# Half of the first product of blocks 3 to 6 as two units of seven block products, with q' and part of k' on ScalarE half a block sooner

## The chip, the cores and the metric

The kernel runs on one core of a Trainium2 chip. The metric is the device time of one execution in microseconds, of which less is better. The engines of the core have queues of their own that run in order: TensorE (PE; its weight loads are listed apart as PEld), VectorE (DVE), ScalarE (ACT), GpSimd (POOL) and SyncE (SP, which only issues DMAs here).

## The reference

Eight batch entries ("blocks" 0 to 7) of 576 tokens go through a linear attention with eight heads of 64, and then through a feed-forward layer of width 2048:

```python
def phi(x, c, s):
    r = np.maximum(x, 0.0)
    return np.concatenate([r * c, r * s], axis=-1)
q_p = phi(q, cos_w, sin_w)          # cos and sin of pi/2 * pos / 576
k_p = phi(k, cos_w, sin_w)
kv = np.einsum('bhsf,bhsd->bhfd', k_p, v)
z = np.sum(k_p, axis=2)
num = np.einsum('bhsf,bhfd->bhsd', q_p, kv)
den = np.einsum('bhsf,bhf->bhs', q_p, z)[..., None] + 1e-06
x = num / den                        # then tokens x 512
...
h = x @ w_in                         # 512 -> 2048: the first product
g = h * (1.0 / (1.0 + np.exp(-1.702 * h)))
out = g @ w_out                      # 2048 -> 512: the second product
```

Inputs and output are float32; matmuls take bfloat16 operands and add up in float32.

## The kernel before, in words

A block is worked in two stages, with the attention of the block after it (`nb`) laid between their matmuls.

**First product.** 512 of a block's tokens (64 of each block go into a common tail, `xt`) are multiplied by `w_in` in 16 chunks of 128 features: `mm1` (L373) is four matmuls of 512 columns into a PSUM bank (L365) and a GELU on ScalarE into `gT` (L371). Near its end `kv_next` (L711) makes k'v of the next block (72 small matmuls, L237) and VectorE copies it out as `kvs` (L245).

**Second product.** It is written as seven products of half-size blocks (`PRODUCTS`, L481) in place of eight: `wino_mm` (L508) does one half of one product, eight matmuls of 256 columns (L519), fourteen times a block. VectorE makes the sums of `g` that they need (`g_sums`, L466) and joins results (`join`, L538); ScalarE copies three of them out (`keep`, L527: "kept" p1, u2, p5) and the last, p4 (L586). Between the halves stand the numerators of the next block (`x_next`, L883: `num_mm` on TensorE, L310, `num_div` on VectorE, and a transposing DMA into `xT`, L354), five a block. The output leaves by DMAs on POOL's queue.

**Operands of the attention.** q' and k' are relu times a weight by position: an instruction with the cosine and one with the sine for each piece. `trig` (L161) does one of nine pieces of k' (128 x 256), `trig_q` (L176) one of five chunks of q' (128 x 512), each on VectorE or, with `act=True`, on ScalarE (L167, L183). A chunk of q' is then turned by a transposing DMA on SP's queue into `qT` (`qturn_dma`, L217). `vcopy` (L187) casts v. In blocks 2 to 6, all of this stood at the start of the first product, on VectorE.

**Units.** In the last block the first product is already done by seven block products in place of eight: class `Unit` (L642). A unit covers four chunks of features; its steps 1, 2, 6, 7, 5, 4, 3 are four matmuls of 256 columns each (L657) into three banks A, Bk and Bp. After steps 1, 6 and 7 ScalarE copies bank A out (`snap`, L669), and the next step into A waits for this copy; after steps 2, 5 and 3 VectorE adds a copy and a bank (`add`, L664); GELUs read the sums. Units need sums of `w_in` (`win_sum`, L614) and of x (`x_sum`, L631).

The order of all instructions is the order in which the kernel's code issues them (a manual schedule). PSUM banks go round: four of pool `pmm`, and two double ones of pool `pat`.

Of the kernel before, what the change touches and what calls it, by code (L numbers as in the profile page):

```python
# [20 lines left out]
def kernel(  # L21
# [230 lines left out]
                         start=first, stop=last)  # L252

    def ksum_rows():
        st["row"] = small.tile([2, 512], BF16, name="row", bufs=1)
        nc.vector.tensor_copy(st["row"], st["ks"][0:2])

    def ksum_turn():
# [27 lines left out]
    def div_half(a):  # L286
        pv = nums["ps"][a][:, 0:260].rearrange("p (h e) -> p h e", h=4)
        inv = small.tile([128, 4], F32, name="invh")
        nc.vector.reciprocal(inv, pv[:, :, 64])
        xn = small.tile([128, 4, 64], BF16, name="xh")  # L290
        nc.vector.tensor_tensor(xn, pv[:, :, 0:64],
                                inv.unsqueeze(2).to_broadcast([128, 4, 64]), op=MUL)
        nums[0, a] = [nums["ps"][a], xn]
# [71 lines left out]
            nc.tensor.matmul(hp[fc][:, t0:t1], wcol(kc, fc), x[b][:, kc, t0:t1],  # L365
                             start=(kc == 0), stop=(kc == KC - 1))

    def gelu(fc):
        if fc % 4 == 0:
            gT[fc // 4] = gpool.tile([128, 4, MT], BF16, name="g")  # L370
        nc.scalar.activation(gT[fc // 4][:, fc % 4], hp.pop(fc), AF.Gelu_apprx_sigmoid)  # L371

# [5 lines left out]

    xt = one.tile([128, KC, B * 64], BF16, name="xt")
    gt = one.tile([128, FC, B * 64], BF16, name="gt")  # L380

    gt5 = gt.rearrange("p f (a b t) -> p f a b t", a=2, t=32)

    def mm1_tail_first(half):
        hps = pmm.tile([128, 8, 64], F32, name="mm")
        for f in range(8):
            for kc in range(KC):
                nc.tensor.matmul(hps[:, f], wcol(kc, half * 8 + f), xt[:, kc, 0:64],  # L388
                                 start=(kc == 0), stop=(kc == KC - 1))
        nc.scalar.activation(gt5[:, ts(half, 8), :, 0], hps.rearrange("p f (a t) -> p f a t", a=2),  # L390
                             AF.Gelu_apprx_sigmoid)

    def mm1_tails(fc):
        hps = pmm.tile([128, MT], F32, name="mm")
# [89 lines left out]
    OPENS = ("p1", "p2", "p5")  # L484
    bank = {}
    kept = {}

    banks = {"main": {}, "tail": {}}

# [10 lines left out]
            banks[which][n, "all"] = t.rearrange("p (c d) -> p c d", c=2) if one_bank else None  # L500

    def wino_open():
        for n in ("w", "x", "y"):
            t = pmm.tile([128, 2, HD], F32, name="mm")
            bank[n] = [t[:, c] for c in range(2)]
            bank[n, "all"] = t
# [18 lines left out]
        eng.dma_start(out=dst[:, 2 * i + c0:2 * i + c1, ts(n, HD)], in_=t[:, c0:c1])  # L525

    def keep(n, src, act=True):  # L527
        kept[n] = ypool.tile([128, 2, HD], F32, name=f"kept_{n}", bufs=1)
        parts = [(kept[n], bank[src, "all"])]
        if bank[src, "all"] is None:  # L530
            parts = [(kept[n][:, c], bank[src][c]) for c in range(2)]
        for o, i in parts:
            if act:
                nc.scalar.activation(o, i, AF.Identity)  # L534
            else:
                nc.vector.tensor_copy(o, i)
# [74 lines left out]
        slot_no[0] += 1  # L611
        return slots[slot_no[0] % 8].rearrange("p (f t) -> p f t", f=2)

    def win_sum(n, i):  # L614
        tt = nc.vector.tensor_tensor
        o = {m: ws[m][:, :, ts(i, 512)] for m in ws}
        a = {(0, k): w_in_t[i][:, ts(k, 2), :] for k in range(2)}
        a.update({(1, k): w_in_t[2][:, ts(k, 2), ts(i, 512)] for k in range(2)})
        if n == "s1":
            tt(o[n], a[1, 0], a[1, 1], op=ADD)  # L620
        elif n == "s2":
            tt(o[n], o["s1"], a[0, 0], op=SUB)
        elif n == "s3":
            tt(o[n], a[0, 0], a[1, 0], op=SUB)
        else:
            tt(o[n], a[0, 1], o["s2"], op=SUB)

    def x_blk(b, k, t):
        return x[b][:, ts(k, 2), ts(t, 256)]

    def x_sum(b, n):  # L631
        tt = nc.vector.tensor_tensor
        if n == "t1":
            tt(xs[n], x_blk(b, 0, 1), x_blk(b, 0, 0), op=SUB)
        elif n == "t2":
            tt(xs[n], x_blk(b, 1, 1), xs["t1"], op=SUB)
        elif n == "t3":
            tt(xs[n], x_blk(b, 1, 1), x_blk(b, 0, 1), op=SUB)
        else:
            tt(xs[n], x_blk(b, 1, 0), xs["t2"], op=SUB)  # L640

    class Unit:  # L642
        def __init__(self, b, u, A, Bk, Bp):
            self.b, self.u = b, u
            self.A, self.Bk, self.Bp = [t.rearrange("p (f t) -> p f t", f=2) for t in (A, Bk, Bp)]

        def mm(self, to, a, t, opens):
            for j in range(2):
                fc = 2 * self.u + j
                for k in range(2):  # L650
                    if isinstance(a, str):
                        lhs = ws[a][:, k, ts(fc // 4, 512)].rearrange("p (f c) -> p f c", c=4)[:, :, fc % 4]
                    else:
                        lhs = wcol(2 * a[1] + k, 8 * a[0] + fc)
                    rhs = xs[t][:, k] if isinstance(t, str) else x_blk(self.b, *t)[:, k]

                    nc.tensor.matmul(to[:, j], lhs, rhs, start=(opens and j == 0 and k == 0), stop=(k == 1),  # L657
                                     skip_group_check=True)
# [3 lines left out]
            nc.scalar.activation(o, i, AF.Gelu_apprx_sigmoid)  # L662

        def add(self, i, j):  # L664
            o = slot()
            nc.vector.tensor_tensor(o, i, j, op=ADD)
            return o

        def snap(self, i):  # L669
            o = slot()  # L670
            nc.scalar.activation(o, i, AF.Identity)
            return o

        def step(self, p):
            if p == 1:
                self.mm(self.A, (0, 0), (0, 0), True)
                self.s1 = self.snap(self.A)
            elif p == 2:
                self.mm(self.Bk, (0, 1), (1, 0), True)
                self.c11 = self.add(self.s1, self.Bk)  # L680
            elif p == 6:
                self.mm(self.A, "s2", "t2", False)
                self.s2 = self.snap(self.A)
            elif p == 7:
                self.mm(self.A, "s3", "t3", False)
                self.s3 = self.snap(self.A)
            elif p == 5:
                self.mm(self.Bp, "s1", "t1", True)
                self.c22 = self.add(self.s3, self.Bp)
            elif p == 4:  # L690
                self.mm(self.A, (1, 1), "nt4", False)
            else:
                self.mm(self.Bp, "s4", (1, 1), False)
                self.c12 = self.add(self.s2, self.Bp)

    def idle(n, cols=512):
        w = pmm.tile([128, 512], F32, name="mm")
# [191 lines left out]
    for b in range(1, B):  # L889
# [1 line left out]
        if nb is None:  # L891
            break
        f0 = 5 if b == 1 else 0
        for fc in range(f0, FC):
            if nb is not None and fc == f0:
                for c in range(5):
                    trig_q(c)
                    qturn_dma(c)
            if nb is not None and fc == f0 + 1:
                kv_operands(nb)  # L900

                if nb + 1 < B:
                    if b == 1:
                        load(kf, k, nb + 1, nc.sync)
                    load_q(nb + 1, nc.sync)
            if fc == 8 and b == 1:
                vcopy()
            if fc == 12:
                if b > 1:
                    g_sums(("s3",), 0)  # L910
                    g_sums(("s3",), 1)
                g_sums(("s1", "s2", "s4") if b > 1 else ("s1", "s2"), 0)
            if fc == 14 and nb is not None and b > 1:
                kv_next()
            mm1(b, fc)
        if nb is not None:
            x_open(nb)
            if b > 1:
                x_next(nb, 0)
            else:  # L920
                kv_mm_next()
            g_sums(("s1", "s2"), 1)
            if b == 1:
                kv_evac(0, 4)
                g_sums(("s3",), 0)
# [3 lines left out]
            for p in range(7):  # L929
                for c in range(2):  # L930
                    wino_mm(p, c)
                    s = 2 * p + c
                    if c == 1:
                        wino_after(b, p)
                    for c2 in at.get(s, ()):
                        x_next(nb, c2)
                        if c2 == 3 and nb + 1 < B:
                            if b > 1:
                                load(kf, k, nb + 1, nc.sync)
                            load(vf, v, nb + 1, nc.sync)  # L940
                    if s == 1 and b > 1:
                        g_sums(("s4",), 1)
                    if s == 2 and b == 1:
                        g_sums(("s3",), 1)
                    if s == 4 and b == 1:
                        g_sums(("s4",), 0)
                    if s == 6 and b == 1:
                        g_sums(("s4",), 1)

    b = B - 1
    for o, i in later:
        nc.gpsimd.dma_start(out=o, in_=i)
    for fc in range(FC):
# [99 lines left out]
```

## Time and profile before

| | us |
|---|---|
| median of 3 runs | 277.93 (277.73 to 277.98) |
| profiled execution, whole time | 277.36 |
| its span in the profile | 275.6 |
| one block, 2 to 6, from chain of waits | 28.6 |
| first product of a block, 64 matmuls of 512 columns | 13.9 |
| second product, 112 matmuls of 256 columns | 12.2 |
| granted TensorE clock | 0.999 |

The span is the time from the first to the last recorded instruction; the whole time has what lies around it too. The page lists busy time by engine and by group of instructions ("line engine op out<-in xcount | busy, mean ns of one | idle before"). The mean of one is longer than the distance between the starts of two, because an engine overlaps instructions that follow one another; distances are read from the timeline.

### The profile page before, as it was taken

Reading aid. Unit: us, or ns where it says so; the run is one execution under the profiler, and the core shown is the slowest. Engines: PE = TensorE matmul, PEld = TensorE weight load, DVE = VectorE, ACT = ScalarE, POOL = GpSimd, SP = SyncE. Lnnn points to the kernel's source line nnn. Section 1 sums busy time; section 2 is a strip of 40 time slices with the busy share of each in tenths; the row PEclk is TensorE's granted clock in tenths of the full one; section 3 lists DMA queues with packets and bytes.
Section 4 is the critical chain, followed back from the end, with each engine's and each line's share of the span. In section 5 each row is a group of like instructions: output and inputs, shape, how many; then the busy total and the mean of one; then the engine's idle time right before and its main releaser. Section 6 shows DMA issues by size and latency. Waiting matters only on the chain.

```text
span 275.6 us, 6720 instructions
## 1 busy us (share of the span) xinstructions
PE 269.3 (98%) x2748; PEld 195.0 (71%) x2748; DVE 199.4 (72%) x478; ACT 133.9 (49%) x237; POOL 41.3 (15%) x70
## 2 busy tenths in 40 slices
PE   7899999999999999999999999999999999999994
PEld 2685645856975698559855895589648976999983
DVE  4843776698899686978698759875987783744741
ACT  6967642574226512652165216621563147677621
POOL 6690000000130012001210012002200162000310
PEclk9999999999999999999999999999999999999999
DMA  7999999999999988998899969978991353000333
GB/s 240 250 211 298 276 293 153 281 300 200 286 213 223 218 170 257 274 171 191 241 285 176 211 194 351 176 190 125 365 245 26 88 167 118 0 2 0 84 109 114
DMA packets 73661, 53.57 MB, mean 194 GB/s; under 512 B 52736, under 2 KB 63488, under 8 KB 73632
## 3 DMA queue, kind: packets, MB, share of 16 engines
q1 hardware_dynamic: 67504, 36.97, 59.6%
q0 software_dynamic: 6128, 16.19, 22.2%
q8 instruction: 21, 0.34, 0.5%
q14 instruction: 8, 0.07, 0.1%
HBM read 36.70 MB, written 9.44 MB: 167 GB/s over the span
## 4 chain that ended last, share of the span: by engine, by line
PE 93%; DMA 4%; DVE 1%; ACT 0%; issue 0%; POOL 0%
PE mm L365 35%; PE mm L519 31%; PE mm L421 5%; PE mm L657 4%; PE at L519 4%; PE mm L396 4%; PE at L237 4%; PE at L310 3%; DMA sums<-in_v_dram 2%; DMA kf<-in_k_dram 1%; PE at L342 1%; PE mm L388 1%; DVE xn L325 1%; PE mm L205 0%; ACT xT L349 0%
## 5 line engine op out<-in xcount | busy, mean ns | idle before, releaser
L365 PE MATMUL mm<-xT,w_in 128*128 128x512 bf16 (+1 forms) x528 | 99.8, 345 | 0.0
L371 ACT ACTIVATE g<-mm 128x512 bf16<-128x512 f32 x112 | 66.0, 598 | 34.8 <-PE mm L365 34.8
L365 PEld LDWEIGHTS <-w_in 128*128 128x128 bf16 x528 | 53.0, 113 | 40.4
L519 PEld LDWEIGHTS <-sums 128*128 128x128 bf16 x448 | 42.5, 98 | 4.7
L525 POOL DMA_DIRECT2D out_dram<-ysb x24 | 17.4, 725 | 183.0 <-DVE den L321 85.4
L519 PE MATMUL mm<-wsum,sums 128*128 128x256 bf16 x336 | 39.9, 272 | 0.0
L519 PEld LDWEIGHTS <-g 128*128 128x128 bf16 x336 | 32.0, 98 | 3.6
L325 DVE TENSOR_TENSOR xn<-at,inv 128x512 bf16<-128x512 f32 x39 | 27.0, 692 | 1.3
L169 DVE TENSOR_SCALAR kr<-kf,cosw 128x256 bf16<-128x256 f32 x69 | 24.1, 349 | 5.2 <-DMA kf<-in_k_dram 5.2
L519 PE MATMUL mm<-w_out_sb,g 128*128 128x256 bf16 x224 | 26.6, 273 | 0.0
L169 DVE TENSOR_SCALAR kr<-kf,sinw 128x256 bf16<-128x256 f32 x68 | 23.0, 339 | 0.0
L534 ACT ACTIVATE kept_p<-mm 128x512 f32<-128x512 f32 (+1 forms) x15 | 8.5, 569 | 20.0 <-PE mm L519 20.0
L185 DVE TENSOR_SCALAR qn<-qf,cosw 128x512 bf16<-128x512 f32 (+1 forms) x33 | 16.4, 497 | 2.3 <-DMA qf<-in_q_dram 2.3
L321 DVE TENSOR_SCALAR den<-at 128x8 f32<-128x8 f32 x36 | 5.9, 163 | 16.5 <-PE at L310 16.5
L586 ACT ACTIVATE ysb<-mm 128x512 f32<-128x512 f32 x6 | 3.6, 598 | 29.0 <-PE mm L519 29.0
L310 PEld LDWEIGHTS <-qT 128*128 128x128 bf16 x312 | 14.3, 97 | 2.4
L310 PE MATMUL at<-kvs,qT 128*128 128x65 bf16 x312 | 15.7, 193 | 0.0
L185 DVE TENSOR_SCALAR qn<-qf,sinw 128x512 bf16<-128x512 f32 (+1 forms) x33 | 15.6, 474 | 0.0
L534 ACT ACTIVATE kept_u<-mm 128x512 f32<-128x512 f32 (+1 forms) x8 | 4.4, 544 | 23.2 <-DVE xn L325 16.8
L421 PE MATMUL mm<-w_out_sb,g 128*128 128x512 bf16 x64 | 14.8, 379 | 0.0
L519 PE MATMUL mm<-wsum,g 128*128 128x256 bf16 x112 | 13.4, 273 | 0.0
L519 PE MATMUL mm<-w_out_sb,sums 128*128 128x256 bf16 x112 | 13.4, 273 | 0.0
(147 smaller groups left out, 319.9 us busy)
## 6 DMA issues: line engine op xcount, KB each, us to landing
kf<-in_k_dram SPq DMA_DIRECT2D x6, 1152.0 KB, 6.3
vf<-in_v_dram SPq DMA_DIRECT2D x6, 1152.0 KB, 11.2
qf<-in_q_dram SPq DMA_DIRECT2D x6, 1024.0 KB, 6.8
out_dram<-ysb POOLq DMA_DIRECT2D x24, 256.0 KB, 7.1
w_out_sb<-in_moe_w_out_dram POOLq DMA_DIRECT2D x4, 512.0 KB, 17.6
kf<-in_k_dram POOLq DMA_DIRECT2D x1, 1152.0 KB, 13.4
vf<-in_v_dram POOLq DMA_DIRECT2D x1, 1152.0 KB, 20.7
w_in<-in_moe_w_in_dram POOLq DMA_DIRECT2D x2, 512.0 KB, 10.0
```

The costliest lines, as they stand in the source:

```text
L169: eng.tensor_scalar(o, i, 0.0, w[:, j:j + 1], op0=MAX, op1=MUL)
L185: nc.vector.tensor_scalar(o, i, 0.0, sc, op0=MAX, op1=MUL)
L237: nc.tensor.matmul(st["kv", i][:, hh, ds(col, n)], kr[r, j, i, :], rhs(r, i, j), start=(j == 0), stop=(j == NS - 1))
L310: nc.tensor.matmul(ps[:, h // 4, ds((h % 4) * 65, 65)], qT[:, h, ts(c, 128)], kvs_of(h), start=not eps_too, stop=(not eps_too or h % 4 == ...
L325: nc.vector.tensor_tensor(xn, pv[:, :, :, 0:64], inv.unsqueeze(3).to_broadcast([128, 2, 4, 64]), op=MUL)
L365: nc.tensor.matmul(hp[fc][:, t0:t1], wcol(kc, fc), x[b][:, kc, t0:t1], start=(kc == 0), stop=(kc == KC - 1))
L371: nc.scalar.activation(gT[fc // 4][:, fc % 4], hp.pop(fc), AF.Gelu_apprx_sigmoid)
L396: nc.tensor.matmul(hps[:, 64:B * 64], wcol(kc, fc), xt[:, kc, 64:B * 64], start=(kc == 0), stop=(kc == KC - 1))
L421: nc.tensor.matmul(yp[b, t, c0][:, c0:c1], w, w_out_sb[:, fc, c0:c1], start=(fc == 0), stop=(fc == FC - 1))
L519: nc.tensor.matmul(bank[to][c], lhs, rhs, start=opens, stop=(fc == HF - 1), skip_group_check=True)
L525: eng.dma_start(out=dst[:, 2 * i + c0:2 * i + c1, ts(n, HD)], in_=t[:, c0:c1])
L534: nc.scalar.activation(o, i, AF.Identity)
```

## The change

In blocks 3 to 6 (`PAIR`) `mm1_pair` takes the place of the sixteen `mm1`. Chunks 4 to 7 and 12 to 15 stay whole; chunks 0 to 3 and 8 to 11 are done by two units, U and V, with steps laid between the whole chunks. Six chunks use a bank of `pat`, two of `pmm`. The sums of `w_in` for the units are made once, in block 2, in the space of `gt`; so the first block's tail goes to `gt0` and is copied into `gt` by POOL at the end. The sums of x are made on VectorE behind the second product of the block before. The units' copies lie in `gt` and in the three kept buffers, which are now fixed.

q' moves from the start of the first product, on VectorE, to ScalarE behind half products 8 to 12 of the second product before it (from block 1 on), with its transposing DMAs; two of nine pieces of k' move with it (for blocks 4 to 7); the other seven are laid between the units' steps. The load of kf comes with that of qf in the first product. Some `g_sums` move.

```diff
@@ gelu, mm1_tail_first
-    def gelu(fc):
-        if fc % 4 == 0:
+    def gelu(fc, units=False):
+        if fc % 4 == 0 and not units:
             gT[fc // 4] = gpool.tile([128, 4, MT], BF16, name="g")
...
+    gt0 = one.tile([128, FC, 64], BF16, name="gt0")
...
-        nc.scalar.activation(gt5[:, ts(half, 8), :, 0], hps.rearrange("p f (a t) -> p f a t", a=2),
-                             AF.Gelu_apprx_sigmoid)
+        nc.scalar.activation(gt0[:, ts(half, 8)], hps, AF.Gelu_apprx_sigmoid)
@@ wino_open
-        for n in ("w", "x", "y"):
+        for n in ("w", "y", "x"):
@@ new
+    PAIR = range(3, B - 1)
...
+    def x_pair(b):
+        t = xpool.tile([128, KC, MT], BF16, name="xT")
+        xp[b] = {n: t[:, i].rearrange("p (k t) -> p k t", k=2) for i, n in enumerate(("t1", "t2", "t3", "nt4"))}
+        for n in xp[b]:
+            x_sum(b, n, xp[b])
+
+    def mm1_at(b, fc):
+        hp[fc] = pat.tile([128, 2, 512], F32, name="at")[:, 0]
+        for kc in range(KC):
+            nc.tensor.matmul(hp[fc], wcol(kc, fc), x[b][:, kc], start=(kc == 0), stop=(kc == KC - 1))
+        gelu(fc, True)
+
+    def mm1_pair(b, nb):
+        for qd in (0, 2, 1, 3):
+            gT[qd] = gpool.tile([128, 4, MT], BF16, name="g")
+        banks4 = [pmm.tile([128, 512], F32, name="mm") for _ in range(4)]
+        U, V = [Unit(b, u, banks4[u], banks4[2], banks4[3], ws_pair, xp[b], pair_slot) for u in range(2)]
+        ks = iter(range(2, NS))
+
+        def k_next(n):
+            for _ in range(n):
+                trig(kr, kf, next(ks))
+
+        U.step(1)
+        V.step(1)
+        k_next(2)
+        mm1_at(b, 4)
+        mm1_at(b, 5)
+        U.step(2)
+        k_next(3)
+        U.step(6)
+        V.step(6)
+        U.gelu(0, 0, U.c11)
+        mm1_at(b, 6)
+        mm1_at(b, 7)
+        V.step(2)
+        k_next(1)
+        U.step(7)
+        U.step(5)
+        V.gelu(0, 0, V.c11)
+        k_next(1)
+        V.step(7)
+        mm1_at(b, 12)
+        U.gelu(1, 1, U.c22)
+        U.step(4)
+        U.gelu(1, 0, U.A)
+        vcopy()
+        if nb + 1 < B:
+            load(kf, k, nb + 1, nc.sync)
+            load_q(nb + 1, nc.sync)
+        U.step(3)
+        V.step(4)
+        V.gelu(1, 0, V.A)
+        U.gelu(0, 1, U.c12)
+        mm1_at(b, 13)
+        g_sums(("s3",), 1)
+        V.step(5)
+        mm1_part(b, 14, 0, MT)
+        V.gelu(1, 1, V.c22)
+        V.step(3)
+        gelu(14)
+        kv_next()
+        mm1_part(b, 15, 0, MT)
+        V.gelu(0, 1, V.c12)
+        gelu(15)
+        g_sums(("s1", "s2"), 0)
@@ the loop over blocks
+        if b in PAIR:
+            mm1_pair(b, nb)
-        for fc in range(f0, FC):
-            if nb is not None and fc == f0:
+        for fc in range(f0, FC) if b not in PAIR else ():
+            if b == 1 and fc == f0:
                 for c in range(5):
                     trig_q(c)
                     qturn_dma(c)
...
-                    if b == 1:
-                        load(kf, k, nb + 1, nc.sync)
+                    load(kf, k, nb + 1, nc.sync)
                     load_q(nb + 1, nc.sync)
+                if b == 2:
+                    for n in ws_pair:
+                        win_sum(n, 0, ws_pair)
...
             g_sums(("s1", "s2"), 1)
+            if b > 2:
+                x_next(nb, 0)
...
                         if c2 == 3 and nb + 1 < B:
-                            if b > 1:
-                                load(kf, k, nb + 1, nc.sync)
                             load(vf, v, nb + 1, nc.sync)
-                    if s == 1 and b > 1:
+
+                    if s > 7 and s < 13 and nb + 1 < B:
+                        trig_q(s - 8, act=True)
+                        qturn_dma(s - 8)
+                        if s > 10 and nb in PAIR:
+                            trig(kr, kf, s - 11, act=True)
+                    if s == 1 and b == 2:
                         g_sums(("s4",), 1)
+                    if s == 1 and b > 2:
+                        g_sums(("s3",), 0)
+                    if s in (2, 4) and b > 2:
+                        g_sums(("s4",), s // 2 - 1)
...
+            if nb in PAIR:
+                x_pair(nb)
...
+    nc.gpsimd.tensor_copy(gt5[:, :, :, 0], gt0.rearrange("p f (a t) -> p f a t", a=2))
     for o, i in later:
```

More of the change, by code (lines that the diff above doesn't have):

```diff
@@ L254, in ksum_rows @@
     def ksum_rows():
-        st["row"] = small.tile([2, 512], BF16, name="row", bufs=1)
+        st["row"] = wsum[0:2, 1, 0:512]
         nc.vector.tensor_copy(st["row"], st["ks"][0:2])
@@ L289, in div_half @@
         nc.vector.reciprocal(inv, pv[:, :, 64])
-        xn = small.tile([128, 4, 64], BF16, name="xh")
+        xn = small.tile([128, 4, 64], BF16, name="xh", bufs=2)
         nc.vector.tensor_tensor(xn, pv[:, :, 0:64],
@@ L486 @@
     kept = {}
+    kept_t = {n: one.tile([128, 2, HD], F32, name=f"kept_{n}") for n in ("p1", "u2", "p5")}
     banks = {"main": {}, "tail": {}}
@@ L527, in keep @@
     def keep(n, src, act=True):
-        kept[n] = ypool.tile([128, 2, HD], F32, name=f"kept_{n}", bufs=1)
+        kept[n] = kept_t[n]
         parts = [(kept[n], bank[src, "all"])]
@@ L612, in slot, with win_sum @@
         return slots[slot_no[0] % 8].rearrange("p (f t) -> p f t", f=2)
-    def win_sum(n, i):
+    def win_sum(n, i, ws=ws):
         tt = nc.vector.tensor_tensor
@@ L629, in x_blk, with x_sum @@
         return x[b][:, ts(k, 2), ts(t, 256)]
-    def x_sum(b, n):
+    def x_sum(b, n, xs=xs):
         tt = nc.vector.tensor_tensor
@@ L642, with __init__ @@
     class Unit:
-        def __init__(self, b, u, A, Bk, Bp):
-            self.b, self.u = b, u
+        def __init__(self, b, u, A, Bk, Bp, ws=ws, xs=xs, slot=slot):
+            self.b, self.u, self.ws, self.xs, self.slot = b, u, ws, xs, slot
             self.A, self.Bk, self.Bp = [t.rearrange("p (f t) -> p f t", f=2) for t in (A, Bk, Bp)]
@@ L651, in mm @@
                     if isinstance(a, str):
-                        lhs = ws[a][:, k, ts(fc // 4, 512)].rearrange("p (f c) -> p f c", c=4)[:, :, fc % 4]
+                        lhs = self.ws[a][:, k, ts(fc // 4, 512)].rearrange("p (f c) -> p f c", c=4)[:, :, fc % 4]
                     else:
                         lhs = wcol(2 * a[1] + k, 8 * a[0] + fc)
-                    rhs = xs[t][:, k] if isinstance(t, str) else x_blk(self.b, *t)[:, k]
+                    rhs = self.xs[t][:, k] if isinstance(t, str) else x_blk(self.b, *t)[:, k]
                     nc.tensor.matmul(to[:, j], lhs, rhs, start=(opens and j == 0 and k == 0), stop=(k == 1),
@@ L664, in add @@
         def add(self, i, j):
-            o = slot()
+            o = self.slot()
             nc.vector.tensor_tensor(o, i, j, op=ADD)
@@ L669, in snap @@
         def snap(self, i):
-            o = slot()
+            o = self.slot()
             nc.scalar.activation(o, i, AF.Identity)
@@ L694, in step, with pair_slot @@
                 self.c12 = self.add(self.s2, self.Bp)
+    PAIR = range(3, B - 1)
+    gt_flat = gt.rearrange("p f e -> p (f e)")
+    ws_pair = {n: gt_flat[:, ts(i, 1024)].rearrange("p (k f) -> p k f", k=2)
+               for i, n in enumerate(("s1", "s2", "s3", "s4"))}
+    pair_slots = [gt_flat[:, 4096:8192].bitcast(F32)[:, ts(i, 512)] for i in range(4)]
+    pair_slots += [kept_t[n].rearrange("p c d -> p (c d)") for n in ("p1", "u2", "p5")]
+    pair_no = [0]
+    xp = {}
+    def pair_slot():
+        pair_no[0] += 1
+        return pair_slots[pair_no[0] % 7].rearrange("p (f t) -> p f t", f=2)
@@ L917 @@
             x_open(nb)
-            if b > 1:
+            if b == 2:
                 x_next(nb, 0)
-            else:
+            if b == 1:
                 kv_mm_next()
             g_sums(("s1", "s2"), 1)
+            if b > 2:
+                x_next(nb, 0)
             if b == 1:
@@ L937 @@
                         if c2 == 3 and nb + 1 < B:
-                            if b > 1:
-                                load(kf, k, nb + 1, nc.sync)
                             load(vf, v, nb + 1, nc.sync)
-                    if s == 1 and b > 1:
+                    if s > 7 and s < 13 and nb + 1 < B:
[4 more added lines that the diff above has]
+                    if s == 1 and b == 2:
                         g_sums(("s4",), 1)
+                    if s == 1 and b > 2:
+                        g_sums(("s3",), 0)
+                    if s in (2, 4) and b > 2:
+                        g_sums(("s4",), s // 2 - 1)
                     if s == 2 and b == 1:
```

## The prediction

> **What bounds the kernel now.** I read the page first, then the chain that ended last, then the timeline of each engine over one block, and last the waits.
>
> ```profile
> span 275.6 us, 6720 instructions
> PE 269.3 (98%) x2748; PEld 195.0 (71%) x2748; DVE 199.4 (72%) x478; ACT 133.9 (49%) x237; POOL 41.3 (15%) x70
> ```
>
> TensorE is busy all the time, so only fewer or shorter matmuls can gain. The chain, in order of time (start, length, what), shows it for block 3; the last line is from block 7, where the unit products exist already:
>
> ```profile
> 108.95 12.09 PE mm L365 x56
> 121.04 1.19 PE at L237 x72
> 122.23 1.85 PE mm L365 x8
> 124.08 0.24 PE at L310 x8
> 124.32 1.75 PE mm L519 x16
> ...
> 132.28 5.24 PE mm L519 x48
> 137.52 12.09 PE mm L365 x56
> ...
> 237.94 0.87 PE mm L657 x8
> ```
>
> A block lasts 28.57 us (108.95 to 137.52) and TensorE has no hole in it: 13.94 us of first product, 1.19 of kv, five numerators of 0.24, 12.24 of second product. No stall waits to be removed; a new one is paid in full. The other engines, block 3, by windows (length, then PE, PEld, DVE, ACT, POOL busy, clock, DMA share):
>
> ```profile
> 108.95:137.52 28.57, 28.57 (x289) 20.49 (x288) 23.05 (x57) 11.94 (x20) 2.90 (x5) 1.00 1.01 225
> ```
>
> VectorE has 5.5 us free, ScalarE 16.6; the DMA engines are full most of the time.
>
> **The matmuls.** A 512-column matmul costs 12.09/56 = 0.216 us, a 256-column one 0.87/8 = 0.109 (L657; L519 has 12.24/112, the same). In blocks 3 to 6 the change replaces 32 of the first kind (6.91) by 2 units x 7 products x 4 = 56 of the second (6.12): 0.79 us less a block, 3.16 in all. The changed program's order on TensorE has these matmuls and nothing else new, so this part does what it says.
>
> Weight loads rise from 32 to 56. In block 7 they take 0.114 us (L657 on w_in, x48), a little more than the 0.109 at which their matmuls follow one another, and the chain shows no hole there: they overlap. The Trainium skill, "TensorE: Matmul & The Clock Gate", section Back-to-back issue gap, says that in a real stream load and matmul together set the spacing and gives 131 ns for 512 columns; the rows here say 216, so its figure does not hold in this kernel. By that figure (an estimate) the 32 matmuls would take 4.2 us, less than the 56 can, and the change could only lose. What its rule would do through the loads is a rival below.
>
> **The ScalarE queue, where I expect the answer.** The queue runs in order. Until now it held three copies and an output copy in the second product. Now, behind the copy "kept p5" (after half product 8 of 14), come 10 instructions of q' and 4 of k', then the output copy of p4, then the copy s1 of unit U, the copy of V, and the GELUs of chunks 4 and 5. TensorE may not start U's second product into bank A (step 6) before s1 is copied out. The rows for each piece, ScalarE's timeline:
>
> ```profile
> 8.32 0.49 ACT L167 ACTIVATE qn<-qf,cosw 128x256 bf16<-128x256 f32 x1
> 8.72 0.49 ACT L167 ACTIVATE qn<-qf,sinw 128x256 bf16<-128x256 f32 x1
> ...
> 35.15 0.72 ACT L183 ACTIVATE qn<-qf,cosw 128x512 bf16<-128x512 f32 x1 [1.01 <-DMA qf<-in_q_dram]
> 35.77 0.71 ACT L183 ACTIVATE qn<-qf,sinw 128x512 bf16<-128x512 f32 x1
> 36.38 0.71 ACT L183 ACTIVATE qn<-qf,cosw 64x512 bf16<-64x512 f32 x1
> ...
> 132.13 0.60 ACT L534 ACTIVATE kept_p<-mm 128x512 f32<-128x512 f32 x1 [1.40 <-PE mm L519]
> ...
> 238.04 0.60 ACT L534 ACTIVATE kept_p<-at 128x512 f32<-128x512 f32 x1 [1.65 <-PE at L519]
> 238.53 1.08 ACT L671 ACTIVATE qn<-mm 128x512 f32<-128x512 f32 x2
> ```
>
> Starts follow one another at 0.615 us (q', (36.38-35.15)/2), 0.40 (the k' form), 0.50 (a copy out of PSUM, 238.53-238.04). With t = 0 at the second product's start (124.32 in block 3):
> - ScalarE: kept p5 starts at 132.13-124.32 = 7.81; q' from 8.31; 10 x 0.615 = 6.15 and 4 x 0.40 = 1.60 bring the output copy to 16.06, s1 of U to 16.56, and its end (0.60) to 17.16.
> - TensorE: the second product ends at 137.52-124.32 = 13.20; step 1 of U and V (8 x 0.109), chunks 4 and 5 (8 x 0.216) and step 2 of U (0.44) bring it to 16.23.
>
> TensorE is 0.93 early. It then starts from a standstill:
>
> ```profile
> 46.74 0.70 DVE xn L325
> 47.45 0.05 issue
> 47.49 0.40 PE at L342 x4
> ```
>
> 0.05 for the signal, and the first 256-column matmul ends 0.27 after its start (L519's mean) where in the stream it is 0.11: 0.21 more. **This wait costs 1.14 us a block**, more than the 0.79 won.
>
> **Smaller waits behind it, per block.** V's step 6 and chunk 6 (it needs chunk 4's bank, freed by a GELU that ends at 17.56+0.60): 0.10. V's step 3 writes the bank that V's add must have read; the trip is 0.16 drain + 0.05 + 0.69 add (L666) + 0.05 = 0.95, with one chunk (0.86) to cover it: 0.09. U's add before V's step 5 stands behind the vcopy of 1.34: 0.09. One chunk, not two, now stands between kv and the numerators, and kvs needs 0.17 + 0.04 + 0.70 (L245) + 0.05 = 0.96: 0.10. Each is an estimate from the rows named, bounded by 0 and about twice its size; no gain is possible in them, since TensorE has no hole now. Sum 0.38.
>
> **What stays hidden.** VectorE loses q' (10 x 0.40) and four instructions of k' (4 x 0.26), and gets 6 adds at 0.60 and 4 sums at 0.42: about even, at most 24 of 28 us. The four sums come after the last join, about t = 12.1 to 13.8, 3 us before step 6 asks for them. win_sum (4 x 0.60, block 2) takes the place of q'. The clearing copy on POOL lies ahead of the late outputs, 9 us before the tail's sums read it. In SP's queue kf now goes out ahead of qf, half a block sooner, vf stays behind the fourth x transpose, and the qT transposes come behind vf instead of after it by a half block; qT is read a full first product later, so it has room. A second load issued behind the first landed 11.2 us after its issue (vf's row on the page). kf goes out when the last k' on VectorE is done, near t = 22.8, 6 us before the next second product; qf is then there about 5 to 6 us into it, and q' asks at 8.3. Cover 2 to 3 us; past it, each us is one us of wait in each of three or four blocks.
>
> **Block 2** keeps its chunks, but ScalarE also does q' in block 1's second product. qf's second part landed at 76.27 in the trace; 6.15 of q' and the output copy end at 83.0, and the fourth chunk asks for that bank at 80.30 + 3 x 0.864 = 82.9. Between 0 and 0.7; I take 0.2.
>
> **The sum.** 4 x (-0.79 + 1.14 + 0.38) + 0.2 = +3.1 us. The profiled execution took 277.36 (span 275.6 and 1.76 around it); it becomes 280.5. The median of the three runs is 277.93, 0.57 above that execution, so I predict 281.0.
>
> **Why q' is dear there.** VectorE does a q' instruction every 0.40 us (L185 in its timeline), ScalarE every 0.615. The Trainium skill, "ScalarE: Activation LUTs", section Rules for kernel authors, puts relu and multiply on VectorE for this reason; by this rule, which the rows bear out, the move loses. Its section on ACT_TABLE_LOAD adds that each [128,1] pointer operand costs about 93 ns; q' has its weight in one. An estimate from that page: with a plain number as scale the 14 instructions would be 1.3 us shorter and the wait gone. No row here shows such a form on q'.
>
> **Rivals.**
> - *ScalarE is in time* (faster). Mechanism: q' at t = 8.3 to 14.5 lies under the second product and s1 is out before 16.2. It decides at q' spacing: (16.23 - 0.60 - 8.31 - 1.60 - 0.50)/10 = 0.52 us. Below it the gain is 0.79 less 0.28 of the trips through VectorE, 4 x 0.51 = 2.0: 275.9. For: ScalarE's 16.6 free us. Against: three spacings at 0.61 to 0.63. Chance 0.11.
> - *Only the bare lateness counts*: 0.93 and nothing more, 4 x 0.14 = 0.6, 278.5. For: small waits often vanish in each other. Against: the restart shown above has both the 0.05 and the drain. 0.13.
> - *qf comes late* by 1 us past its cover: +4 on the forecast, 285. For: DMA share 1.01. Against: the cover of 2 to 3 us. 0.10.
> - *Weight loads bind*: unit matmuls at 0.114, not 0.109; 56 x 0.005 = 0.3 a block, 282.1. The rule of the TensorE page named above goes this way. Against: the 0.87 for 8 in block 7. 0.03.
> - The forecast has 0.63; its own range is 279.3 (the one wait alone) to 282.8 (small waits doubled).
>
> **How the numbers follow.** About 0.2% (0.56 us) is what a measurement can tell from no change. Faster 0.12: the first rival and a little for what I haven't seen. Same 0.08: over half of the second rival, which lies on the edge. Slower 0.80: the rest. The range 277.2 to 284.5 leaves out the first rival and half of the third, with what lies beyond: 0.18.
>
> **What the changed profile would show.** Right: the chain in blocks 3 to 6 no longer all TensorE, with ScalarE pieces (the trig lines, ysb, the copy s1) some 3 us after each second product; a TensorE hole near 1 us in front of step 6, and a block of 29.2 to 29.4 us. Unit products at 0.87 for 8. Wrong on the main step: kept p5 to s1 under 8.4 us, or no hole there; wrong in another way if q' waits for qf, or if the hole stands in front of step 1.

## The result, and the profile after

| | before | after |
|---|---|---|
| median, run alternately | 277.89 (277.59 to 277.98, 5 runs) | 280.86 (280.48 to 280.94, 5 runs) |
| profiled execution, whole time | 277.36 | 280.48 |
| one block, 3 to 6 | 28.57 | 29.23 to 29.30 |
| granted TensorE clock | 0.999 | 1.00 in every block |

The changed kernel takes 1.0101 times as long (95% interval 1.0088 to 1.0113): 2.97 us slower by the medians, 3.12 by the profiled executions, of which 2.9 lie in the span. The page of the changed kernel, span and engines:

```profile
span 278.5 us, 6996 instructions
PE 268.9 (97%) x2844; PEld 204.7 (74%) x2844; DVE 198.2 (71%) x456; ACT 177.5 (64%) x327; POOL 43.0 (15%) x71
```

PE is busy 0.4 us less, although the span is 2.9 longer: TensorE now has holes. ScalarE has 43.6 us more work. The chain that ended last, which used to run through all blocks on TensorE, now breaks off, followed back, at a ScalarE piece in front of block 6's step 6:

```profile
200.22 0.49 ACT gt L672
200.71 0.04 issue
200.75 1.08 PE mm L658 x8
201.83 1.77 PE at L721 x8
203.60 1.75 PE mm L658 x16
```

`gt` (L672) is the copy s1 of unit U, and the eight matmuls behind it are step 6 of U and of V. The last line settles the weight loads: 16 unit matmuls in 1.75 us are 0.109 each, as forecast. Who releases TensorE, by its waits (total, times, longest):

```profile
PE mm L658 <- ACT gt L672: 1.8, 2, 0.9
PE mm L658 <- ACT kept_p L672: 1.7, 2, 0.9
```

Four waits in four blocks, all on copies by `snap`. Block by block, in windows from step 6 to the next step 6 (length, then PE, PEld, DVE, ACT, POOL busy, clock, DMA share, GB/s):

```profile
112.93:142.16 29.23, 28.37 (x312) 22.91 (x312) 22.91 (x53) 21.44 (x41) 2.90 (x5) 1.00 0.97 211
142.16:171.46 29.30, 28.38 (x313) 22.90 (x312) 22.83 (x53) 21.44 (x41) 2.91 (x5) 1.00 0.85 220
171.46:200.75 29.29, 28.38 (x312) 22.92 (x312) 22.82 (x53) 21.43 (x41) 2.90 (x5) 1.00 0.92 211
```

ScalarE is busy 21.4 of 29.3 us in the block, so it is by no means full; what counts is when its work stands in its queue. ScalarE's timeline, from the copy kept p5 to s1, in front of block 3:

```profile
103.60 0.60 ACT L535 ACTIVATE kept_p<-mm 128x512 f32<-128x512 f32 x1 [1.40 <-PE mm L520]
104.10 0.71 ACT L183 ACTIVATE qn<-qf,cosw 128x512 bf16<-128x512 f32 x1
104.71 0.71 ACT L183 ACTIVATE qn<-qf,sinw 128x512 bf16<-128x512 f32 x1
...
111.42 0.49 ACT L167 ACTIVATE kr<-kf,sinw 128x256 bf16<-128x256 f32 x1
111.82 0.57 ACT L587 ACTIVATE ysb<-mm 128x512 f32<-128x512 f32 x1
112.30 1.06 ACT L672 ACTIVATE gt<-mm 128x512 f32<-128x512 f32 x2
```

From kept p5 to s1 it takes 112.30 - 103.60 = 8.70 us (forecast 16.56 - 7.81 = 8.75), without a gap. TensorE's timeline in the same block:

```profile
111.43 0.60 PE L658 MATMUL mm<-xT,w_in 128*128 128x256 bf16 x4
112.93 1.08 PE L658 MATMUL mm<-xT,gt 128*128 128x256 bf16 x8 [0.90 <-ACT gt L672]
113.89 1.89 PE L721 MATMUL at<-xT,w_in 128*128 128x512 bf16 x8
...
119.53 1.03 PE L721 MATMUL at<-xT,w_in 128*128 128x512 bf16 x4
120.57 0.60 PE L658 MATMUL mm<-xT,gt 128*128 128x256 bf16 x4
121.00 1.03 PE L365 MATMUL mm<-xT,w_in 128*128 128x512 bf16 x4
122.00 0.60 PE L658 MATMUL mm<-xT,gt 128*128 128x256 bf16 x4
```

Starts are compared with the stream. Step 2 of U (111.43) would be followed at 111.43 + 4 x 0.109 = 111.87; step 6 starts at 112.93: a hole of **1.06 us** (1.01 in block 4, 1.06 to 1.07 in the others; the 0.90 in the bracket counts from the modelled end of step 2). The eight matmuls of step 6, of U and of V, then take 0.96 (112.93 to 113.89) where the stream takes 0.87: 0.09. A chunk at 119.53 takes 0.864; V's step 5 starts 1.04 later: 0.18. V's step 3 starts 1.00 behind the chunk at 121.00: 0.135. The first numerator starts 0.96 behind chunk 15 (123.72 to 124.68), 0.096 more than a chunk takes; in the kernel before that step costs 0.024, so 0.07 is new. These three have no bracket: holes this short show only in the starts.

### The profile page after: what moved, and what is told of

Its sections match the earlier page's. It is cut to its first block, busy times and chain, and to the rows that moved or that the text cites. A ratio compares the mean times of both kernels' runs of the same rounds, so it can differ in the third digit from the quotient of the medians.

```text
span 278.5 us, 6996 instructions
## 1 busy us (share of the span) xinstructions
PE 268.9 (97%) x2844; PEld 204.7 (74%) x2844; DVE 198.2 (71%) x456; ACT 177.5 (64%) x327; POOL 43.0 (15%) x71
## 5 line engine op out<-in xcount | busy, mean ns | idle before, releaser
L365 PE MATMUL mm<-xT,w_in 128*128 128x512 bf16 (+1 forms) x304 | 51.4, 320 | 0.0
L371 ACT ACTIVATE g<-mm 128x512 bf16<-128x512 f32 x56 | 32.1, 597 | 14.6 <-PE mm L365 14.6
L169 DVE TENSOR_SCALAR kr<-kf,cosw 128x256 bf16<-128x256 f32 x61 | 21.6, 354 | 5.1 <-DMA kf<-in_k_dram 5.1
L721 PE MATMUL at<-xT,w_in 128*128 128x512 bf16 x96 | 23.3, 379 | 0.0
L658 PE MATMUL mm<-xT,gt 128*128 128x256 bf16 x128 | 17.4, 272 | 3.6 <-ACT gt L672 1.8
L169 DVE TENSOR_SCALAR kr<-kf,sinw 128x256 bf16<-128x256 f32 x60 | 20.7, 344 | 0.0
L183 ACT ACTIVATE qn<-qf,cosw 128x512 bf16<-128x512 f32 (+1 forms) x27 | 19.2, 711 | 1.0 <-DMA qf<-in_q_dram 1.0
L658 PEld LDWEIGHTS <-gt 128*128 128x128 bf16 x128 | 14.1, 113 | 7.3 <-issue 6.3
L183 ACT ACTIVATE qn<-qf,sinw 128x512 bf16<-128x512 f32 (+1 forms) x27 | 19.1, 709 | 0.0
L658 PE MATMUL mm<-xT,w_in 128*128 128x256 bf16 x128 | 18.5, 273 | 0.0
```

Of the source, the lines that this page charges most:

```text
L169: eng.tensor_scalar(o, i, 0.0, w[:, j:j + 1], op0=MAX, op1=MUL)
L183: nc.scalar.activation(o, i, AF.Relu, scale=sc)
L721: nc.tensor.matmul(hp[fc], wcol(kc, fc), x[b][:, kc], start=(kc == 0), stop=(kc == KC - 1))
```

## The experiments

The theory: ScalarE's queue is late for s1, by the 14 moved instructions, and TensorE waits for it in each of four blocks; the small waits behind the adds come on top. The rivals: qf or other transfers, the units' own dependences, the small waits alone. Diffs are against the changed kernel. Medians of the kernel before beside these runs lay from 277.64 to 277.83.

### k' back on VectorE

```diff
-        ks = iter(range(2, NS))
+        ks = iter(range(0, NS))
-        k_next(2)
+        k_next(4)
-                        if s > 10 and nb in PAIR:
-                            trig(kr, kf, s - 11, act=True)
```

> All nine pieces of k' go back to VectorE (four of them ahead of U's first add, where VectorE waits); ScalarE keeps q'. Theory A (the ScalarE queue holds up step 6): four instructions of 0.40 us less bring the end of the copy s1 from 0.93 us late to 0.67 us early, so the hole of 1.06 us a block goes: 280.9 - 4 x 1.06 = 276.6, under the kernel before. Rival B (step 6 waits for VectorE's sums, or the units are dear by themselves): the hole stays or grows by VectorE's 1.05 us more a block, 280.9 to 284. Rival C (the earlier loads of kf and qf, and the earlier transposes, are what is late): 280.9, no change.

Measured: 275.96 (275.8 to 277.46, 6 runs), ratio to the kernel before 0.9947 (0.9929 to 0.9966). TensorE's timeline:

```profile
111.29 0.60 PE L658 MATMUL mm<-xT,w_in 128*128 128x256 bf16 x4
111.73 1.04 PE L658 MATMUL mm<-xT,gt 128*128 128x256 bf16 x8
```

0.44 from start to start: the hole before step 6 is gone, and with it 4.9 us by the medians (4.6 by the profiled executions, of which the holes are 4.2; another 0.09 a block is the time that V's step 6 and chunk 6 lost behind it, which is gone too). Four ScalarE instructions of 0.40 a block turn the sign of the whole change. The holes of 0.18 and 0.135 are still there.

### One and three pieces of k' on ScalarE

A dose beside none (above) and two (the change); first one piece, then three:

```diff
-        ks = iter(range(2, NS))
+        ks = iter(range(1, NS))
-        k_next(2)
+        k_next(3)
-                        if s > 10 and nb in PAIR:
-                            trig(kr, kf, s - 11, act=True)
+                        if s > 11 and nb in PAIR:
+                            trig(kr, kf, s - 12, act=True)
```

```diff
+        ks = iter(range(3, NS))
+        k_next(1)
+                        if s > 9 and nb in PAIR:
+                            trig(kr, kf, s - 10, act=True)
```

> One piece of k' on ScalarE, as the step between e1 (none) and the change (two). Theory A: two instructions of 0.40 us less than the change leave 1.06 - 0.80 = 0.26 us of the hole: e1 + 4 x 0.26 = 277.0. If only the bare lateness counted (no 0.21 us for a restart), 0.13 us would be left and e1 + 0.5 = 276.5 come out. Rival B or C: as e1, 276.0.

> Three pieces of k' on ScalarE instead of two, so two instructions of 0.40 us more in front of the copy s1. Theory A: the hole grows by the full 0.80 us in each of the four blocks, 280.9 + 3.2 = 284.1. Rival B: VectorE has 0.53 us less to do, so 280.9 or a little under. Rival C: no change, 280.9.

| pieces | time, us | ratio to the kernel before | hole before step 6 |
|---|---|---|---|
| 0 | 275.96 | 0.9947 (0.9929 to 0.9966) | 0 |
| 1 | 277.40 | 0.9987 (0.9974 to 1.0) | 0.27 in three blocks, 0.22 in block 4 |
| 2 | 280.86 | 1.0101 (1.0088 to 1.0113) | 1.01 in block 4, else 1.06 to 1.07 |
| 3 | 283.93 | 1.0223 (1.0209 to 1.0236) | 1.81 in block 4, else 1.86 to 1.87 |

With three pieces TensorE shows:

```profile
113.62 1.08 PE L658 MATMUL mm<-xT,gt 128*128 128x256 bf16 x8 [1.70 <-ACT gt L672]
```

From one piece to two and from two to three the hole grows by 0.80 us, which is two instructions of 0.40: the wait is paid in full and in a straight line. With one piece the 0.27 fits the 0.26 forecast with a restart, not the 0.13 without. The time came out 0.4 us above the 277.0 forecast; V's step 6 and chunk 6 come late again too, 0.09 a block. Block 4 with one piece shows the restart alone, in TensorE's and ScalarE's timelines:

```profile
140.06 0.60 PE L658 MATMUL mm<-xT,w_in 128*128 128x256 bf16 x4
140.71 1.08 PE L658 MATMUL mm<-xT,gt 128*128 128x256 bf16 x8
```

```profile
140.07 0.58 ACT L672 ACTIVATE kept_p<-mm 128x512 f32<-128x512 f32 x1
```

The copy s1 (here into `kept_p`) ends at 140.66, just as step 2 of U does, and still step 6 starts 0.65 behind the start of step 2 in place of 0.436: 0.22 of hole without any lateness by the ends.

### Shorter ScalarE instructions

Nothing is moved. The moved instructions of q' and k' get a plain number as scale in place of the pointer to the weights; the weighting by position is left out there.

```diff
+            if act == "plain":
+                nc.scalar.activation(o, i, AF.Relu, scale=0.5)
...
-                        trig_q(s - 8, act=True)
+                        trig_q(s - 8, act="plain")
...
-                            trig(kr, kf, s - 11, act=True)
+                            trig(kr, kf, s - 11, act="plain")
```

> The moved q' and k' instructions on ScalarE take a plain number as scale in place of the column of position weights (so the weighting by position is left out for these); their number, order, operands in memory and waits are the same. An estimate from the Trainium skill, ScalarE: Activation LUTs, section What ACT_TABLE_LOAD costs, is 93 ns less for each of the 14. Theory A: then the copy s1 ends 1.30 us sooner, before TensorE asks, and the hole of 1.06 us goes: 276.6; if the instructions do not get shorter, 280.9 and nothing is learned. Rivals B and C: 280.9, since nothing moves on VectorE or in the DMA queues.

Measured: 276.15 (275.91 to 276.49, 5 runs), ratio 0.9943 (0.9932 to 0.9955). ScalarE's timeline:

```profile
103.76 0.60 ACT L539 ACTIVATE kept_p<-mm 128x512 f32<-128x512 f32 x1 [1.40 <-PE mm L524]
104.25 4.25 ACT L185 ACTIVATE qn<-qf 128x512 bf16<-128x512 f32 x8
...
111.15 1.06 ACT L676 ACTIVATE gt<-mm 128x512 f32<-128x512 f32 x2
```

s1 comes 7.39 us behind kept p5 in place of 8.70, and the hole is gone. Instructions, order and transfers are the same as in the change, so it was the length of the queue.

### The move without the units

`PAIR` is empty: all chunks whole, with q' and two pieces of k' on ScalarE and the loads as in the change. The sums of `w_in` are left out, and the sums of `g` and the first numerator stand where the kernel before has them.

```diff
-    PAIR = range(3, B - 1)
+    PAIR = range(0)
...
-        for j in range(NS):
+        for j in range(2 if b > 3 else 0, NS):
...
-                        if s > 10 and nb in PAIR:
+                        if s > 10 and nb > 2:
...
```

> The move alone: q' and two pieces of k' on ScalarE behind the half products, loads and transposes where the change puts them, but all 16 chunks whole, without units. Theory A: ScalarE is as late as with units (the output copy near t = 16.1), but behind it stand only GELUs, which chunks 4 and later need after t = 16.6, and the bank of the output copy is asked for at 15.8, so at most 0.9 us a block: 277.9 to 281; if the hole shows it stands before chunk 3. Rival B: 277.9, no hole. Rival C (the DMAs' new places cost): above 280.

Measured: 282.07 (281.88 to 282.31, 4 runs), ratio 1.0156 (1.0142 to 1.0169). TensorE's timeline:

```profile
112.75 1.46 PE L365 MATMUL mm<-xT,w_in 128*128 128x512 bf16 x6 [0.87 <-ACT ysb L587]
```

The late queue does harm without any unit: here the fourth chunk waits for the bank that the output copy frees, 1.03 us in three blocks and 1.31 in block 4. The place of the hole was forecast, its size not (at most 0.9). By the number alone rival C (above 280) would fit as well, but the four holes, 4.4 us, are the whole loss, and in front of each ScalarE works without a gap for 8.2 us from kept p5 to the output copy, as in the change; no transfer holds it up. The units are not the cause; by the two ratios the change is 0.5% better than the move alone.

### The units without the move

q' stays on VectorE, at the start of the first product, with all of k'.

```diff
+        for c in range(5):
+            trig_q(c)
+            qturn_dma(c)
...
-        ks = iter(range(2, NS))
+        ks = iter(range(0, NS))
-        k_next(2)
+        k_next(4)
...
-                    if s > 7 and s < 13 and nb + 1 < B:
+                    if s > 7 and s < 13 and nb + 1 < B and nb not in PAIR:
...
-                        if s > 10 and nb in PAIR:
-                            trig(kr, kf, s - 11, act=True)
```

> The units alone: q' of blocks 3 to 6's first product stays on VectorE at its start, as in the kernel before, with its transposes, and all of k' is on VectorE; nothing of them is on ScalarE. Theory A: step 6 no longer waits for ScalarE, but VectorE's queue has 4.0 us of q' and 2.1 us of k' in front of U's first add, which ends near t = 20.5 instead of 17.9; V's step 2 into the same bank waits for it, and about 16 us of VectorE's work no longer fit the 14.5 us of the first product: 2 to 3 us a block more than with k' alone on VectorE, 284 to 289. Rival (the units are cheap wherever q' is): 276.

Measured: 286.74 (286.33 to 286.81, 4 runs), ratio 1.0311 (1.0292 to 1.0331). VectorE's and TensorE's timelines:

```profile
109.37 0.48 DVE L185 TENSOR_SCALAR qn<-qf,cosw 128x512 bf16<-128x512 f32 x1
...
115.43 0.68 DVE L667 TENSOR_TENSOR gt<-gt,mm 128x512 f32<-128x512 f32 x1
```

```profile
116.16 0.60 PE L658 MATMUL mm<-xT,w_in 128*128 128x256 bf16 x4 [1.51 <-DVE gt L667]
```

Ten instructions of q' (3.96 us) and four pieces of k' (2.10) stand ahead of U's first add, and TensorE waits 1.7 us for it in three of the four blocks and 2.4 in block 4, and loses 0.66 more a block at V's step 5. So the units need q' off VectorE at that place, and moving q' was no mistake; it was four instructions of k' too many.

### q' three half products sooner

```diff
+                    q0 = 5 if b > 1 else 8
-                    if s > 7 and s < 13 and nb + 1 < B:
-                        trig_q(s - 8, act=True)
+                    if s >= q0 and s < q0 + 5 and nb + 1 < B:
+                        trig_q(s - q0, act=True)
...
-                        if s > 10 and nb in PAIR:
-                            trig(kr, kf, s - 11, act=True)
+                        if s > q0 + 2 and nb in PAIR:
+                            trig(kr, kf, s - q0 - 3, act=True)
```

> Same instructions on ScalarE as in the change, two pieces of k' among them, but q' begins behind half product 5 in place of 8 (from block 2 on), so that ScalarE's idle time between the copies u2 and p5 is used; qf landed 6.2 us into the second product in the changed kernel's trace (131.15 against 124.9). Theory A (what counts is only when the queue is done, not how much ScalarE does): 1.5 us earlier, the hole goes, 276.6. Rival (ScalarE's total work, or qf, is the limit): qf is not there before t = 6.2 to 8, then 278 to 281, with q' waiting for the DMA.

Measured: 277.05 (275.66 to 279.9, 12 runs), ratio 0.9965 (0.9948 to 0.9982). No hole before step 6 is left, but ahead of block 6 there is another. ScalarE's and TensorE's timelines:

```profile
189.07 0.72 ACT L183 ACTIVATE qn<-qf,cosw 128x512 bf16<-128x512 f32 x1 [1.66 <-DMA qf<-in_q_dram]
```

```profile
192.16 1.91 PE L520 MATMUL mm<-w_out_sb,sums 128*128 128x256 bf16 x16 [1.40 <-ACT kept_p L535]
```

q' now asks before qf has landed, kept p5 stands behind it, and p3 waits for the bank. Both theories had a part: the queue is cured, and the rival on qf comes alive where the change still had some 2 us of cover. The runs spread over 4 us; I put that down to qf, but it was not shown run by run.

### The small waits: moving vcopy and V's step 3

vcopy goes behind `U.step(3)` and `V.step(3)` behind `kv_next()`, with k' as in the change, and then with k' on VectorE.

```diff
-        vcopy()
         if nb + 1 < B:
...
         U.step(3)
+        vcopy()
...
-        V.step(3)
         gelu(14)
         kv_next()
+        V.step(3)
```

> The changed kernel with three instructions moved against the small waits alone: vcopy behind U's step 3 and its add, and V's step 3 behind kv, so that kv and chunk 15 cover the trips through VectorE. ScalarE's queue is as in the change. Theory A (the small holes of 0.18, 0.14 and 0.07 us are trips through VectorE and add to the large one): 4 x 0.39 = 1.5 us less than the changed kernel, 279.3, with the hole of 1.06 still there. Rival: the small waits vanish into others when one is moved (the late ScalarE queue sets the pace of the whole first product): 280.9.

> All of k' on VectorE (as in e1) and the moved instructions (as in e5) together. Theory A: both kinds of hole go and all of the 0.79 us a block is kept: 277.9 - 3.2 = 274.7, 1.3 under e1. Rival: VectorE, with 1.05 us more to do a block, is now the one that comes late, and the time stays at e1's 276.0 or above.

Measured: 281.98 (281.45 to 283.17, 5 runs), ratio 1.0156 (1.0131 to 1.0181), and 277.42 (276.98 to 278.41, 12 runs), ratio 0.9984 (0.9972 to 0.9997). Both missed, on the same new hole. With k' on VectorE, its timeline and TensorE's:

```profile
125.02 0.69 DVE L473 TENSOR_TENSOR sums<-g 128x1024 bf16<-128x1024 bf16 x1 [0.70 <-ACT g L663]
...
128.12 0.69 DVE L325 TENSOR_TENSOR xn<-at,inv 128x512 bf16<-128x512 f32 x1
```

```profile
128.96 0.40 PE L310 MATMUL at<-kvs,qT 128*128 128x65 bf16 x8 [0.56 <-DVE den L321]
```

The three holes of 0.18, 0.135 and 0.07 have gone, as meant. But V's last GELU now ends later, four sums wait for it ahead of the first division, and that division (`xn` at 128.12) frees the bank of the third numerator: 0.73 us a block in place of 0.385. The bracket names `den` of the second division, which ended last before the wait; that the first one is meant is shown below, where moving it takes this hole away.

vcopy moved alone, with k' on VectorE:

> All of k' on VectorE, as in e1, and vcopy alone moved behind U's step 3 and its add (V's step 3 stays where the change has it). Theory A (the hole of 0.18 us in front of V's step 5 is vcopy ahead of U's add): it goes and nothing else changes, since the end of the first product and VectorE's start into the second stay as in e1: 276.0 - 4 x 0.18 = 275.3. Rival (vcopy, later, delays what follows it on VectorE): 276.0 or above.

Measured: 278.11 (277.71 to 278.42, 12 runs), ratio 1.0007 (0.9996 to 1.0019). VectorE's and TensorE's timelines:

```profile
119.17 1.35 DVE L193 CAST vt<-vf 128x2304 bf16<-128x2304 f32 x1
120.44 0.68 DVE L477 TENSOR_TENSOR sums<-g 128x1024 bf16<-128x1024 bf16 x1
121.04 0.68 DVE L667 TENSOR_TENSOR kept_p<-gt,mm 128x512 f32<-128x512 f32 x1
```

```profile
121.77 0.60 PE L658 MATMUL mm<-xT,gt 128*128 128x256 bf16 x4 [0.64 <-DVE kept_p L667]
```

vcopy and a sum now stand ahead of V's add instead of U's: the 0.18 is gone, and V's step 3 loses 0.81 in place of 0.135. Missed again, and for the rival's reason.

### Following the wait to its end

To the version with both moves and k' on VectorE: the first division ahead of the four sums, and then also the sums s4 two half products later.

```diff
-        g_sums(("s1", "s2"), 0)
...
-            g_sums(("s1", "s2"), 1)
             if b > 2:
                 x_next(nb, 0)
+                g_sums(("s1", "s2"), 0)
+            g_sums(("s1", "s2"), 1)
```

> As e6 (all of k' on VectorE, vcopy and V's step 3 moved), and on VectorE the first numerator's division now stands ahead of the sums s1 and s2 of both halves. Theory A (e6's hole of 0.73 us in front of the third numerator is its PSUM buffer, which the first division frees, and that stood behind four sums): the hole goes, and so do the small ones of the first product: 277.4 - 4 x 0.73 = 274.5. Rival (the sums, now 1.1 us later, hold up the third product): the hole moves there and the time stays near 277.

```diff
-                    if s in (2, 4) and b > 2:
-                        g_sums(("s4",), s // 2 - 1)
+                    if s in (4, 6) and b > 2:
+                        g_sums(("s4",), s // 2 - 2)
```

> As e10, with the sums s4 two half products later on VectorE (behind the third and fourth divisions), so that the third division, which frees the fifth numerator's PSUM buffer, comes 0.6 us sooner. Theory A (e10's hole of 0.29 us in front of the fifth numerator is that buffer): it goes, and no TensorE hole above 0.1 us is left in blocks 3 to 6: 276.0 - 4 x 0.29 = 274.8. Rival (s4, later, holds up the product p3, which reads it): the hole moves there, 276.

Measured: 275.98 (275.76 to 276.26, 6 runs), ratio 0.9929 (0.9911 to 0.9948), with 0.29 us left ahead of the fifth numerator; then **274.32** (274.06 to 275.12, 5 runs), ratio 0.9883 (0.9866 to 0.9899). Windows of the last one, from step 6 to step 6:

```profile
111.86:139.64 27.78, 27.78 (x315) 22.98 (x314) 23.48 (x55) 19.86 (x37) 2.90 (x4) 1.00 1.07 227
139.64:167.41 27.77, 27.77 (x315) 22.96 (x313) 24.21 (x58) 19.76 (x37) 2.90 (x4) 1.00 1.05 225
```

PE is busy through the whole block again, and the block lasts 28.57 - 0.79 = 27.78: the gain in matmuls to the last hundredth. This version beats both kernels, by 1.2% and (by the two ratios) 2.2%.

## Why the prediction was right

**The matmuls.** -0.79 a block was forecast; the last experiment shows it bare (27.78 against 28.57).

**The ScalarE queue.** Forecast 1.14 a block, measured 1.01 to 1.07. The forecast takes its moments from the chain, which goes by the ends of matmuls, so the terms are compared there. In block 6, s1 ends at 200.71, and step 2 of U ended 0.90 before step 6 starts at 200.75: 0.86 late, forecast 0.93 (the queue from kept p5 to s1 came out 0.05 shorter). The restart is the forecast one, 0.04 to the start and a first matmul that ends 0.27 behind it where the stream has 0.11, in all 0.20 against 0.21; block 4 with one piece of k' shows it bare. That the late queue is the cause is shown four ways: less work in it (no piece, one piece), more work (three), the same work shorter, and the queue without the units. The forecast's turning point, a q' spacing of 0.52 us with k' as it is, was not tested by itself: with the plain scale q' comes every 0.52, but the four k' instructions are shorter too.

The Trainium skill, "ScalarE: Activation LUTs", section What ACT_TABLE_LOAD costs, from which the 1.3 us were estimated, agrees with the trace: 1.31 us for 14 instructions, 0.094 each. The Trainium skill's rule that relu and multiply belong on VectorE ("ScalarE: Activation LUTs", section Rules for kernel authors) holds by the time of an instruction, 0.40 against 0.615. By place it does not hold with the units: q' ahead of their adds on VectorE cost 286.74, q' on ScalarE with all of k' on VectorE 275.96.

**The small waits.** Forecast 0.38, measured 0.48; the causes were the forecast ones, the sizes were off both ways. V's step 6 and chunk 6 lost 0.09 (forecast 0.10): V's copy ends at 113.36 and the GELU of chunk 4 at 113.84, each 0.05 before the matmul that waits for it. U's add behind vcopy cost 0.18, twice its estimate, V's step 3 0.135, half as much again, and kvs 0.07, two thirds.

**Block 2.** Mis-sized: 0.2 was forecast and nothing came. qf landed some 0.3 us after ScalarE asked (its bracket before the first q' at 75.90), the output copy ended at 82.62, and the fourth chunk found its bank free.

**qf's cover.** qf landed 6.2 us into block 3's second product (131.15 against 124.92), 4.3 and 4.4 into those of blocks 4 and 5, around the 5 to 6 forecast. The forecast of no wait was right, with about 2 us to spare in block 3; the run with q' sooner shows where that ends.

**The sum.** By the windows a block is 0.66 to 0.73 us longer than before, 4 x 0.70 = 2.8 in all (forecast 4 x 0.73 = 2.9; the measured terms add up to 0.74 a block); the rest of the span adds 0.1 and the time around the span 0.2: 3.1, as forecast. So exact a sum is partly luck: the small waits are 0.10 a block over their forecast and the large wait 0.08 under it, and the 0.2 around the span, not foreseen, stands in for the 0.2 of block 2. (The upper end of the forecast's own range, 282.8, is by its terms 282.6.) None of the rivals happened: in the bare lateness there is neither restart nor small wait, and both are there; unit matmuls follow one another at 0.109, so weight loads do not bind; qf was in time.

## What to carry over

An engine that is free for a quarter of the time (ScalarE here: busy 21.4 of 29.3 us) can still be the bound: find in its queue the one short instruction that TensorE waits for (here a copy out of PSUM), add up what stands ahead of it, and compare that moment with the time TensorE needs it; here four instructions of 0.40 us decided between 0.5% faster and 1.0% slower. A small wait in a full schedule is not always removed by moving the one step: here it went to the next bank three times, and had to be followed until the step that got later had slack. Count such waits from start to start, since the short ones carry no bracket.

## What was unexpected

- The small waits could not be taken away one by one. Moving vcopy removed 0.18 and brought 0.81 in place of 0.135; moving V's step 3 with it removed 0.385 and brought 0.73. It took four moves (k', vcopy with V's step 3, the division, s4) until all were gone; other choices of moves were not tried.
- A copy that ends just when the matmuls before it do is already late: with one piece of k', in block 4, s1 and step 2 end together, and the hole is 0.22. In the stream the next matmul starts 0.16 before the one ahead ends (0.27 long, 0.109 apart), and a release takes 0.05 more.
- Issuing one of q's transposing DMAs held SP's queue 1.3 us in places and up to 4.2 us in others (its issue at 107.91 in the changed kernel), with the loads of kf and qf behind it in the queue. The kernel before shows the like: five of them take 12.4 us there from 108.78, and 12.2 in the changed kernel from 106.54. No wait came of it here.
